# One product of q moved last, a closing bank of three steps instead of two, and w_mod loads spread over four iterations

## The chip, the cores and the metric

The kernel runs on one core of one Trainium2 chip. The metric is the time of one execution on the device in microseconds (us). Three runs of the kernel before the change took 440.44, 440.65 and 440.71 us; their median is 440.65 us. TensorE (PE) multiplies, VectorE (DVE) and ScalarE (ACT) do elementwise work, GpSimd (POOL) does small work and issues the accumulating DMAs, SyncE (SP) issues the plain ones. Nearly every wait below is one of these engines waiting for another, or for a DMA.

## The reference

One transformer block with adaLN conditioning: six vectors come from `silu(c) @ w_mod`, then a linear attention and a token-mixing MLP, each behind a modulated layer norm, are added to x. x is 2048 x 448, the hidden size of the MLP is 1792.

```
mod = (_silu(c) @ w_mod).reshape(c.shape[0], 6, 1, -1)
sa, ca, ga, sb, cb, gb = (mod[:, 0], ..., mod[:, 5])
h = _layernorm(x) * (1 + ca) + sa
x = x + ga * _A_ref(h, A_wqkv, A_wo)      # q, k, v; phi(t) = where(t>0, t+1, exp(t)) + 1e-6
h = _layernorm(x) * (1 + cb) + sb         # A: o = phi(q) (phi(k)^T v) / (phi(q) sum phi(k)), then @ wo
x = x + gb * _B_ref(h, B_w1, B_b1, B_w2, B_b2)   # B: gelu(LN(h)^T w1 + b1) w2 + b2, over tokens
```

## The kernel before

**Precision by parts.** PE works on operands rounded to a shorter form. Each f32 operand is cut into a high part (ACT copies it rounded) and a low part (full minus high), and a product becomes high x high, high x low and low x high, summed in one bank of PSUM. The low part is made in two ways: DVE subtracts, or ACT writes the negated high part and POOL issues a DMA that adds the full tile to it (an accumulating DMA). Names ending in h and l are such parts: `hh`, `hl` of the transposed normed tile, `wh`, `wl` of a weight, `pkh`, `pkl` of phi(k), `xh`, `xl` of the normed tile.

**The first stage** goes over the 16 token tiles of 128 rows (numbered from 0; the change's "tile 2" is the second tile, number 1 in the code). A head written out by hand treats tiles 0 to 2, then the loop at L594 runs t from 3 to 15. In iteration t PE makes k of tile t (`project`, eleven matmuls of 448 columns at L356), the transposes of tile t+1 (L325), and `a_outer(t - 3)`: phi(k)^T times the normed tile, eleven matmuls into four banks `cacc` (L453). `a_outer` reads `pkl` of tile t-3. That part is made in `a_pk_parts`, called with t-1 in iteration t: ACT writes the negated high part (L431) and POOL issues the adding DMA (L432). So `pkl` of tile 7 is issued in iteration 8 and read in iteration 10. POOL issues three accumulating DMAs in most iterations: `xl` (L404), `pkl` (L432) and the running sum of phi(k) into `pk` (L438); between them stand its small `rs` operations (L302), the reciprocal deviations of the norm.

**q of tile 1** is `project(1, 0, "qp", True)` at L582. With `late_low` its eleven products are sorted by a key: high x high weight chunks first, then low x high weight, then high x low weight (`wl0_0`, `wl0_1`, `wl0_2`), and at the end the two products of chunk 3, whose lower half holds both parts. `wl0_0` is made with an accumulating DMA (L226), `wl0_1` and `wl0_2` and the low rows of `wh0_3` by DVE (L213, L215).

**SP's queue.** SP issues the loads in the order of the code. A load waits for the last reader of the buffer that it is to fill; the buffers come from one pool of 76 slots, and whatever stands behind a waiting load in SP's queue waits too. In iteration t, `load_x(t + 4)` is issued, and in iterations 10 and 11 the four quarter loads of w_mod's vectors 4 and 3 (`load_mod`, L113). These vectors are used by DVE from iteration 11 on (L181, L183).

**The end.** The token mixer's second matrix is applied by `mult7` in blocks of seven steps. Each step multiplies by h with 448 columns (L1028) and by l with 224 (L1029). Of the very last block, the last `LAST = 2` steps go to a bank of their own, `yl` (`last7`, L1038): three matmuls of 224 columns each (L1043). DVE then adds both halves of the first bank `y` and the bank `yl` to the x tile `xb` (L1045, three additions), and SP stores it (L1046). Ahead of these three, DVE has the same kind of work for the block before: L1055 once and L1060 twice.

Of the kernel before, what the change touches and what calls it, by code (L numbers as in the profile page):

```python
# [30 lines left out]
DVE_LOW = (0, 1, 13, 14, 15)  # L31
AHEAD = 8
LAG = 5
LAST = 2
PRE2 = {16: (1, 0), 12: (1, 1), 8: (1, 2), 3: (4, 3), 1: (4, 4)}
MOD_AT = {11: [(4, 0)], 12: [(4, 1)], 13: [(4, 2)], 14: [(4, 3)], 15: [(3, 0), (3, 1)]}
QS = {0: 2, 4: 2}
WARM = 9
ACT_STATS = ()
PRE = 9  # L40
# [7 lines left out]
def block_kernel(ctx: ExitStack, tc: tile.TileContext, x, wqkv, wo, w1, b1, w2, b2, c, wmod, out):  # L48
# [26 lines left out]
    def bank(name):  # L75
        return psum.tile([P, 512], F32, name=name, tag="bank")
# [30 lines left out]

    wm = {}

    def load_mod(j):  # L110
        for k in range(4):
            wm[j, k] = (tslot if j == 5 else slot)(f"wm{j}_{k}", parts=G)
            nc.sync.dma_start(wm[j, k], wmod[k * G:(k + 1) * G, j * D:(j + 1) * D])  # L113

# [26 lines left out]
    def keep_warm(n):  # L141
        for i in range(n):
            nc.tensor.matmul(warm[:, :P], ones, ones, start=True, stop=True)
# [3 lines left out]
    nc.tensor.transpose(ct, c_sb, ident[:4, :4])  # L147
    keep_warm(WARM)

# [25 lines left out]
    def mod_part(j, k):  # L175
        if k == 0:
            macc[j] = (tslot if j == 5 else slot)(f"acc{j}", parts=G)
            if j == 5:
                nc.scalar.activation(macc[j], wm[j, 0], AF.Copy, scale=sc[:, 0:1])
            else:  # L180
                nc.vector.tensor_scalar_mul(macc[j], wm[j, 0], sc[:, 0:1])  # L181
        else:
            nc.vector.scalar_tensor_tensor(macc[j], wm[j, k], sc[:, k:k + 1], macc[j], op0=ALU.mult, op1=ALU.add)  # L183
# [12 lines left out]
    def mod_sum2(j):  # L196
        ps = bank(f"modp{j}")
        hi, lo = macc.pop(j)
        nc.tensor.matmul(ps[:, :D], ones_r[:G, :], hi, start=True, stop=False)
        nc.tensor.matmul(ps[:, :D], ones_r[:G, :], lo, start=False, stop=True)  # L200
        return ps
# [90 lines left out]
    def a_stats(t, b6=None):  # L292
        if t in ACT_STATS:
            a_rstd(t, a_mean(t))
            return
        b6 = a_moments(t) if b6 is None else b6
        mv = small.tile([P, 2], F32, name=f"mv{t}", tag="mv")
        nc.vector.bn_aggr(mv, b6)
        ve = small.tile([P, 1], F32, name=f"ve{t}", tag="ve")
        nc.vector.tensor_scalar_add(ve, mv[:, 1:2], EPS)  # L300
        rs = small.tile([P, 1], F32, name=f"rs{t}", tag="rs")
        nc.gpsimd.tensor_tensor(rs, ve, mhalf[:, 0:1], op=ALU.pow)  # L302
        st[t] = (mv[:, 0:1], rs)

    def a_norm_a(t):
        h = slot(f"h{t}", 512)
        nc.vector.scalar_tensor_tensor(h[:, :D], X[t], st[t][0], mods[1],
                                       op0=ALU.add if t in ACT_STATS else ALU.subtract, op1=ALU.mult)
        hs[t] = h

    def a_norm_b(t, sa=None):
        h = hs[t]
        nc.vector.scalar_tensor_tensor(h[:, :D], h[:, :D], st.pop(t)[1], mods[0] if sa is None else sa,
                                       op0=ALU.mult, op1=ALU.add)
# [6 lines left out]
    def a_transpose(t):  # L321
        h = hs[t]
        tps[t] = bank(f"tp{t}")
        for ch in range(4):
            nc.tensor.transpose(tps[t][:, ch * P:(ch + 1) * P], h[:, ch * P:(ch + 1) * P], ident)  # L325

    def a_split(t):
        hh = slot(f"hh{t}", 512, F32R)
        hl = slot(f"hl{t}", 512, F32R)
        split(tps.pop(t), hh, hl)  # L330
        heads[t] = (hh, hl)
# [11 lines left out]
    def project(t, j, name, late_low=False):  # L343
        hh, hl = heads[t]
        ps = bank(f"{name}{t}")
        o = ps[:, :D]
        todo = []
        for ch in range(4):
            a, b = (hh, ch, Whi[j, ch]), (hl, ch, Whi[j, ch])
            todo += [a, b] if ch == 3 else [a, (hh, ch, Wlo[j, ch]), b]  # L350
        if late_low:
            ws = [Wlo[j, ch] for ch in range(3)]
            key = lambda m: 3 if m[1] == 3 else 2 if any(m[2] is w for w in ws) else 0 if m[0] is hh else 1
            todo.sort(key=key)
        for n, (a, ch, b) in enumerate(todo):
            nc.tensor.matmul(o, a[:, ch * P:(ch + 1) * P], b, start=(n == 0), stop=(n == 10))  # L356
        return o
# [3 lines left out]
    def a_exp(t, ps):  # L361
        eks[t] = (slot(f"ek{t}"), slot(f"rk{t}"))
        nc.scalar.activation(eks[t][0], ps, AF.Exp)
        nc.scalar.activation(eks[t][1], ps, AF.Relu)
# [20 lines left out]
    def a_q(t):  # L385
        qps[t] = project(t, 0, "qp")
        del heads[t]

    def a_phi_q(keep=0):
        for t in sorted(qps)[:len(qps) - keep]:  # L390
            phi_q(qps.pop(t), f"q{t}", t)
            if t > QLATE:
                phi_q_sum(t)
# [21 lines left out]
    def a_high(t):  # L415
        a_high_act(t)
        a_high_low(t)
# [3 lines left out]
    def a_pk(t, ps):  # L421
        pkf[t] = phi_k(t, ps, tslot if t < 2 else slot)
# [21 lines left out]
    def a_outer(t):  # L444
        if not cacc:
            cacc.extend(bank(f"cacc{ch}") for ch in range(4))
        xh, xl = xss.pop(t)
        kh, kl = pks.pop(t)
        for ch in range(4):
            s = slice(ch * P, (ch + 1) * P)  # L450
            todo = [(xh, kh), (xh, kl)] + ([(xl, kh)] if ch < 3 else [])
            for i, (a, b) in enumerate(todo):
                nc.tensor.matmul(cacc[ch][:, :D], a[:, s], b, start=(t == 0 and i == 0),  # L453
                                 stop=(t == NT - 1 and i == len(todo) - 1))
# [139 lines left out]
    for t in range(3, NT):  # L594
        kp = project(t, 1, "kp")
        if t + 1 < NT:
            a_transpose(t + 1)
        a_outer(t - KV_LAG)
        if t in Q_EARLY:
            a_q(t)  # L600
        if t == 10:
            mp = mod_sum2(2)
        if t + 1 < NT:
            a_split(t + 1)
        if t + 2 < NT:
            a_norm_a(t + 2)

        for j, i in MOD_AT.get(t, ()):
            mod_part(j, i)
        if 11 <= t < 15:  # L610
            nc.vector.tensor_mul(wo_sb[t - 11], wo_sb[t - 11], mods[2][:G])
        a_exp(t, kp)
        if t + 2 < NT:
            a_norm_b(t + 2)
        a_pk(t, kp)
        a_phi_q()
        a_pk_parts(t - 1)
        if t + 3 < NT:
            a_stats(t + 3)
        if t + 2 < NT:  # L620
            a_dup(t + 2)
        if t == 3:
            a_high(3)
            a_high(4)
        if t + 2 < NT:
            a_high(t + 2)
        if t == 10:
            mod_out(2, mp)
        if t + 4 < NT:
            load_x(t + 4)  # L630
        if 5 <= t < 9:
            mod_part(2, t - 5)
        if t == 9:
            mod_split(2)
        if 5 <= t <= 5 + QLATE:
            phi_q_sum(t - 5)
        if t in (10, 11):
            load_mod(14 - t)
        if t == 4:
            for g in range(4):  # L640
                w = tslot(f"wo{g}", parts=G)
                nc.sync.dma_start(w, wo[g * G:(g + 1) * G, :])
                wo_sb.append(w)
            load_qkv(2, tslot)
            b1c = cst.tile([P, NF], F32, name="b1c")
            nc.sync.dma_start(b1c, b1.rearrange("(k p) -> p k", p=P))
            b2c = cst.tile([P, NT], F32, name="b2c")
            nc.sync.dma_start(b2c, b2.rearrange("(k p) -> p k", p=P))
        load_to(PRE_LOAD.get(t, 0))
# [205 lines left out]
    for i in range(NT + LAG):  # L855
# [6 lines left out]
        if 0 <= i - 1 < NT:  # L862
            b_out(i - 1)
        nq = min(len(late), QS.get(i, 1))
        for _ in range(nq):
            a_q(late.pop(0))
        t = i - LAG
# [146 lines left out]
    def mult7(q, m, r0, r1):  # L1014
# [6 lines left out]
        for r in range(r0, r1):  # L1021
            (h, l), i = hilo[q, m][r // 4], r % 4
            w, wh = uops[b, r]
            s = slice(i * P, (i + 1) * P)
            if (q, m) == (NP - 1, 6) and r >= PAIRS - LAST:
                last.append((h[:, s], l[:, s], w))
                continue
            nc.tensor.matmul(ps[:, :D], h[:, s], w, start=opens and r == r0, stop=False, skip_group_check=True)  # L1028
            nc.tensor.matmul(ps[:, :HD], l[:, s], wh, start=False,  # L1029
                             stop=closes and r == PAIRS - 1 - (LAST if (q, m) == (NP - 1, 6) else 0),  # L1030
                             skip_group_check=True)
# [6 lines left out]
    def last7():  # L1038
        x = X[NT - 1][:, :HD]
        ps = bank("yl")[:, :HD]  # L1040
        for i, (h, l, w) in enumerate(last):
            for n, (a, b) in enumerate(((h, w[:, :HD]), (h, w[:, HD:]), (l, w[:, :HD]))):
                nc.tensor.matmul(ps, a, b, start=i + n == 0, stop=n == 2 and i == LAST - 1)  # L1043
        for s in (acc2[NP - 1, 0][:, :HD], acc2[NP - 1, 0][:, HD:D], ps):
# [72 lines left out]
    k = NT  # L1117
# [24 lines left out]
    for o0, n in W1G[1:]:  # L1142
# [5 lines left out]
        for r in range(first, NT):  # L1148
# [4 lines left out]
            if xleft and k % 2:  # L1153
                t = xleft.pop(0)
# [11 lines left out]
    for q, m, r0, r1 in order:  # L1166
        if jobs:
            jobs.pop(0)()
        while xleft:
            t = xleft.pop(0)  # L1170
# [41 lines left out]
```

## Time and profile before

| what | value |
|---|---|
| median of 3 runs | 440.65 us (440.44 to 440.71) |
| the profiled execution | 440.77 us, of which the span from its first to its last instruction is 439.1 us |
| busy: PE, DVE, ACT, POOL | 433.9, 365.1, 266.9, 119.3 us |
| mean granted TensorE clock | 1.000 |
| DMA packets | 64.51 MB, mean 147 GB/s over the span |

Busy time is the time in which an engine's instructions run; waiting and issuing are not in it. Matmuls overlap: a row gives the duration of one, and the distance between two starts is shorter. The chain of waits follows the program back from its last instruction, at each step to what released it. A row of the timeline gives start, duration, engine, line, operation, output<-inputs, shape and count, and in brackets the idle time of that engine just before and what ended it. The view of windows gives for stretches of time each engine's busy time, the clock, the busy share of the DMA engines and what they moved; packets that overlap on an engine are both counted, so the share can be somewhat above 1.

### The profile page before, as it was taken

How to read it: one execution, taken by the hardware profiler on the slowest of the kernel's cores; microseconds unless marked ns; L12 is line 12 of the kernel's file. 1: busy time of each engine (PE TensorE's matmuls, PEld its weight loads, DVE VectorE, ACT ScalarE, POOL GpSimd, SP SyncE). 2: the span in 40 equal slices, each digit the busy share in tenths (PEclk: the TensorE clock that was granted, in tenths of full speed). 3: DMA queues.
4: the chain of work that ended last, by engine and by line, in shares of the span. 5: the costliest groups of instructions: out<-in, count | busy, mean ns of one | idle time of the engine just before them, and what ended most of it. 6: DMA issues, size and time to landing. Idle time of an engine off the chain costs nothing.

```text
span 439.1 us, 7288 instructions
## 1 busy us (share of the span) xinstructions
PE 433.9 (99%) x2394; PEld 402.4 (92%) x2394; DVE 365.1 (83%) x792; ACT 266.9 (61%) x570; POOL 119.3 (27%) x196
## 2 busy tenths in 40 slices
PE   8999999999999999999999999999999999999996
PEld 7689999999899999999999999999999999999996
DVE  5996898988898999997469586439999998898894
ACT  3778877655657777776766254236675555655550
POOL 2205775520024455664300000010112230231110
PEclk9999999999999999999999999999999999999999
DMA  8987999993441224222427546476667977977531
GB/s 233 303 213 117 181 197 230 221 258 102 138 100 26 47 47 123 50 50 60 132 69 237 177 143 186 131 194 187 151 143 191 177 172 176 188 161 208 75 52 34
DMA packets 65022, 64.51 MB, mean 147 GB/s; under 512 B 8472, under 2 KB 56792, under 8 KB 64984
## 3 DMA queue, kind: packets, MB, share of 16 engines
q1 hardware_dynamic: 54608, 47.62, 36.8%
q0 software_dynamic: 10368, 16.42, 23.8%
q8 instruction: 19, 0.31, 0.3%
q14 instruction: 19, 0.16, 0.1%
q10 hardware_dynamic: 8, 0.00, 0.0%
HBM read 41.88 MB, written 7.34 MB: 112 GB/s over the span
## 4 chain that ended last, share of the span: by engine, by line
PE 95%; DMA 3%; DVE 1%; ACT 0%; issue 0%; SPq 0%; DVEq 0%
PE y L1028 19%; PE up L829 10%; PE up L828 10%; PE up L830 10%; PE y L1029 9%; PE op L778 8%; PE cacc L453 8%; PE qp L356 7%; PE kp L356 7%; DMA wl<-wr 2%; PE tq L758 2%; PE tp L325 1%; DMA wm<-in_w_mod_dram 1%; PE kvb L691 1%; PE wp L846 1%; PE colp L475 0%
## 5 line engine op out<-in xcount | busy, mean ns | idle before, releaser
L829 PE MATMUL up<-h2l,ph 128*128 128x448 f32 x224 | 81.3, 363 | 0.0
L828 PE MATMUL up<-h2h,ph 128*128 128x448 f32 x224 | 81.2, 362 | 0.0
L830 PE MATMUL up<-h2h,pl 128*128 128x448 f32 x224 | 80.7, 360 | 0.0
L988 POOL DMA_DIRECT2D a<-a x16 | 14.1, 948 | 145.5 <-DMA a<-in_B_w_dram 97.8
L828 PEld LDWEIGHTS up<-h2h,ph 128*128 128x128 f32 x224 | 42.0, 188 | 3.3
L830 PEld LDWEIGHTS up<-h2h,pl 128*128 128x128 f32 x224 | 41.9, 187 | 3.0
L829 PEld LDWEIGHTS up<-h2l,ph 128*128 128x128 f32 x224 | 42.0, 188 | 2.1
L80 DVE TENSOR_TENSOR pl<-pr,ph 128x512 fp32r<-128x512 f32 x48 | 32.3, 686 | 11.5 <-ACT ph L79 8.6
L79 ACT ACTIVATE ph<-pr 128x512 fp32r<-128x512 f32 x48 | 29.1, 627 | 17.8 <-PE up L829 7.4
L1050 ACT ACTIVATE cc<-y 128x448 f32<-128x448 f32 x24 | 13.0, 544 | 22.9 <-PE y L1029 22.9
L453 PE MATMUL cacc<-pkh,xh 128*128 128x448 f32 x64 | 24.3, 379 | 0.0
L453 PE MATMUL cacc<-pkl,xh 128*128 128x448 f32 x64 | 23.2, 363 | 0.0
L778 PE MATMUL op<-oh,pth 128*128 128x448 f32 x60 | 23.0, 383 | 0.0
L1071 POOL DMA_DIRECT2D out_dram<-yt x14 | 12.9, 921 | 34.9 <-DVE yt L1057 25.4
L778 PE MATMUL op<-oh,ptl 128*128 128x448 f32 x60 | 21.7, 362 | 0.0
L356 PE MATMUL qp<-wh,hh 128*128 128x448 f32 x60 | 21.6, 365 | 0.0
L356 PE MATMUL qp<-wh,hl 128*128 128x448 f32 x60 | 21.4, 362 | 0.0
L356 PE MATMUL kp<-wh,hl 128*128 128x448 f32 x56 | 20.3, 363 | 0.0
L356 PE MATMUL kp<-wh,hh 128*128 128x448 f32 x56 | 20.2, 362 | 0.0
L736 POOL TENSOR_SCALAR den<-den 128x16 f32<-128x16 f32 x16 | 8.6, 536 | 39.2 <-DVE den L733 39.1
L763 ACT ACTIVATE pth<-tq 128x512 fp32r<-128x512 f32 (+1 forms) x16 | 9.6, 599 | 15.7 <-PE tq L758 15.6
L302 POOL TENSOR_TENSOR rs<-ve,mhalf 128x1 f32<-128x1 f32 x16 | 13.9, 869 | 18.8 <-DVE ve L300 18.5
(234 smaller groups left out, 1356.9 us busy)
## 6 DMA issues: line engine op xcount, KB each, us to landing
pr<-in_B_w_dram SPq DMA_DIRECT2D x56, 256.0 KB, 2.9
a<-in_B_w_dram SPq DMA_DIRECT2D x32, 256.0 KB, 4.3
a<-in_B_w_dram SPq DMA_DIRECT2D x32, 192.0 KB, 4.2
wm<-in_w_mod_dram SPq DMA_DIRECT2D x24, 196.0 KB, 4.9
x<-in_A_x_dram SPq DMA_DIRECT2D x16, 224.0 KB, 4.0
out_dram<-x SPq DMA_DIRECT2D x14, 224.0 KB, 2.0
out_dram<-yt POOLq DMA_DIRECT2D x14, 224.0 KB, 4.5
pk<-pk POOLq DMA_DIRECT2D x12, 224.0 KB, 4.7
```

Of the source, the lines that this page charges most:

```text
L79: nc.scalar.activation(hi, full, AF.Copy)
L80: nc.vector.tensor_sub(lo, full, hi.bitcast(F32))
L302: nc.gpsimd.tensor_tensor(rs, ve, mhalf[:, 0:1], op=ALU.pow)
L356: nc.tensor.matmul(o, a[:, ch * P:(ch + 1) * P], b, start=(n == 0), stop=(n == 10))
L453: nc.tensor.matmul(cacc[ch][:, :D], a[:, s], b, start=(t == 0 and i == 0), stop=(t == NT - 1 and i == len(todo) - 1))
L778: nc.tensor.matmul(opb[t][:, :D], a[:, g * P:(g + 1) * P], b, start=(n == 0), stop=(n == len(todo) - 1))
L828: nc.tensor.matmul(ps[:, :D], hi[:, sl], mh, start=first, stop=False)
L829: nc.tensor.matmul(ps[:, :D], hi[:, sl], ml, start=False, stop=False)
L830: nc.tensor.matmul(ps[:, :D], lo[:, sl], mh, start=False, stop=last)
L988: nc.gpsimd.dma_start(w, a, accum_op=ALU.add)
L1028: nc.tensor.matmul(ps[:, :D], h[:, s], w, start=opens and r == r0, stop=False, skip_group_check=True)
L1029: nc.tensor.matmul(ps[:, :HD], l[:, s], wh, start=False, stop=closes and r == PAIRS - 1 - (LAST if (q, m) == (NP - 1, 6) else 0), skip_gro ...
```

## The change

Three edits that don't touch each other. A constant more stands at the top, so lines from 38 on move down by one.

```diff
-LAST = 2
+LAST = 3
...
+MOD_LOAD = {8: (4, (0, 1)), 9: (4, (2, 3)), 10: (3, (0, 1)), 11: (3, (2, 3))}
...
-    def load_mod(j):
-        for k in range(4):
+    def load_mod(j, ks=range(4)):
+        for k in ks:
             wm[j, k] = (tslot if j == 5 else slot)(f"wm{j}_{k}", parts=G)
...
-            key = lambda m: 3 if m[1] == 3 else 2 if any(m[2] is w for w in ws) else 0 if m[0] is hh else 1
+            key = lambda m: 3 if m[1] == 3 else 4 if m[2] is ws[0] else 2 if any(m[2] is w for w in ws) else 0 if m[0] is hh else 1
...
-        if t in (10, 11):
-            load_mod(14 - t)
+        if t in MOD_LOAD:
+            load_mod(*MOD_LOAD[t])
```

**q of tile 1, on PE** (output `qp1`; `wh0_c`, `wl0_c` are the high and low parts of q's weight chunk c, `hh1` and `hl1` those of the tile). Before:

```order
L356 MATMUL qp1_403<-wh0_2_295,hl1_263 128x448
L356 MATMUL qp1_403<-wl0_0_272,hh1_262 128x448
L356 MATMUL qp1_403<-wl0_1_314,hh1_262 128x448
L356 MATMUL qp1_403<-wl0_2_357,hh1_262 128x448
L356 MATMUL qp1_403<-wh0_3_297,hh1_262 128x448
L356 MATMUL qp1_403<-wh0_3_297,hl1_263 128x448
L356 MATMUL qp2_427<-wh0_0_270,hh2_324 128x448
```

and now:

```order
L357 MATMUL qp1_403<-wh0_2_295,hl1_263 128x448
L357 MATMUL qp1_403<-wl0_1_314,hh1_262 128x448
L357 MATMUL qp1_403<-wl0_2_357,hh1_262 128x448
L357 MATMUL qp1_403<-wh0_3_297,hh1_262 128x448
L357 MATMUL qp1_403<-wh0_3_297,hl1_263 128x448
L357 MATMUL qp1_403<-wl0_0_272,hh1_262 128x448
L357 MATMUL qp2_427<-wh0_0_270,hh2_324 128x448
```

The product with `wl0_0` moves from the seventh place to the eleventh; the four behind it move up by one. The next projection, `qp2`, starts at the same place.

**The loads in SP's queue** (`x12` to `x15` are token tiles, `wm4_k` and `wm3_k` the quarters of w_mod's vectors 4 and 3). Before:

```order
L106 DMA x12_930<-in_A_x_dram 128x448
L106 DMA x13_995<-in_A_x_dram 128x448
L106 DMA x14_1067<-in_A_x_dram 128x448
L113 DMA wm4_0_1069<-in_w_mod_dram 112x448
L113 DMA wm4_1_1071<-in_w_mod_dram 112x448
L113 DMA wm4_2_1073<-in_w_mod_dram 112x448
L113 DMA wm4_3_1075<-in_w_mod_dram 112x448
L106 DMA x15_1141<-in_A_x_dram 128x448
L113 DMA wm3_0_1143<-in_w_mod_dram 112x448
L113 DMA wm3_1_1145<-in_w_mod_dram 112x448
L113 DMA wm3_2_1147<-in_w_mod_dram 112x448
L113 DMA wm3_3_1149<-in_w_mod_dram 112x448
```

and now:

```order
L107 DMA x12_930<-in_A_x_dram 128x448
L114 DMA wm4_0_933<-in_w_mod_dram 112x448
L114 DMA wm4_1_935<-in_w_mod_dram 112x448
L107 DMA x13_999<-in_A_x_dram 128x448
L114 DMA wm4_2_1005<-in_w_mod_dram 112x448
L114 DMA wm4_3_1007<-in_w_mod_dram 112x448
L107 DMA x14_1075<-in_A_x_dram 128x448
L114 DMA wm3_0_1077<-in_w_mod_dram 112x448
L114 DMA wm3_1_1079<-in_w_mod_dram 112x448
L107 DMA x15_1145<-in_A_x_dram 128x448
L114 DMA wm3_2_1147<-in_w_mod_dram 112x448
L114 DMA wm3_3_1149<-in_w_mod_dram 112x448
```

`x13` has two w_mod loads ahead of it that it did not have and `x14` four; between `x14` and `x15` stand two instead of four, and two instead of four come behind `x15`. Because the loads ask for buffers earlier, most buffers of the pool go to other tiles from iteration 8 to 15. In the changed program `wm4_0` takes the buffer that phi(k) of tile 4 (`pk4`) leaves, and waits for the sum DMA (L438) that reads it; `wm4_1` takes that of the normed tile `h7` and waits for the `xl` DMA of tile 7; `x13` waits for a matmul of PE's `a_outer(4)`; `wm4_2` takes that of `h8` and waits for the `xl` DMA of tile 8; `x14` and `wm3_0` take those of the two inputs of phi(k) of tile 8 (DVE, L369), `wm3_1` one that DVE leaves in the same iteration.

**The end, on PE** (`y_0` is the first bank, `yl` the closing one; the left operand is the moving half of u, the right the weight part). Before:

```order
L1029 MATMUL y_0_5394<-ut_3_3677,a22l_0_5463 128x224
L1028 MATMUL y_0_5394<-ut_4_3811,a22h_4_5466 128x448
L1029 MATMUL y_0_5394<-ut_4_3811,a22l_4_5467 128x224
L1043 MATMUL yl<-ut_5_3934,a22h_4_5466 128x224 x2
L1043 MATMUL yl<-ut_5_3934,a22l_4_5467 128x224
L1043 MATMUL yl<-ut_6_4057,a22h_4_5466 128x224 x2
L1043 MATMUL yl<-ut_6_4057,a22l_4_5467 128x224
```

and now:

```order
L1030 MATMUL y_0_5394<-ut_3_3677,a22l_0_5463 128x224
L1044 MATMUL yl<-ut_4_3811,a22h_4_5466 128x224 x2
L1044 MATMUL yl<-ut_4_3811,a22l_4_5467 128x224
L1044 MATMUL yl<-ut_5_3934,a22h_4_5466 128x224 x2
L1044 MATMUL yl<-ut_5_3934,a22l_4_5467 128x224
L1044 MATMUL yl<-ut_6_4057,a22h_4_5466 128x224 x2
L1044 MATMUL yl<-ut_6_4057,a22l_4_5467 128x224
```

The first bank closes one step earlier; that step is now three matmuls of 224 columns in the closing bank, in place of one of 448 and one of 224. The order on DVE, ACT and POOL does not change.

## Prediction

> **What bounds the kernel now.** I read the page's busy times and the chain of waits first.
>
> ```profile
> PE 433.9 (99%) x2394; PEld 402.4 (92%) x2394; DVE 365.1 (83%) x792; ACT 266.9 (61%) x570; POOL 119.3 (27%) x196
> PE 95%; DMA 3%; DVE 1%; ACT 0%; issue 0%; SPq 0%; DVEq 0%
> ```
>
> PE is busy for 433.9 of 439.1 us and 95% of the chain is PE's. So an edit can gain only where PE stands still, and a stop that it adds is paid in full to the end, since PE has no idle time in which to catch up. The chain's one long DMA, in order of time:
>
> ```profile
> 17.43 8.12 DMA wl<-wr
> ...
> 25.60 3.48 PE qp L356 x16
> ```
>
> The low part `wl0_0` of q's first weight chunk lands at 17.43 + 8.12 = 25.55, and PE goes on at 25.60. That is the wait which the new order of q avoids. The other edits work at 50 to 78 us (loads) and in the last 3 us.
>
> **q of tile 1.** PE's timeline there:
>
> ```profile
> 24.75 0.77 PE L356 MATMUL qp<-wh,hl 128*128 128x448 f32 x3
> ...
> 25.60 0.88 PE L356 MATMUL qp<-wl,hh 128*128 128x448 f32 x3
> 26.31 0.36 PE L356 MATMUL qp<-wh,hh 128*128 128x448 f32 x1
> ...
> 26.71 0.36 PE L356 MATMUL qp<-wh,hh 128*128 128x448 f32 x1
> ```
>
> Running matmuls start 0.20 apart (26.31 to 26.71 is two). The three from 24.75 could be followed by the next at 24.75 + 3 x 0.20 = 25.35; it came at 25.60, a stop of 0.25. The three behind it took 26.31 - 25.60 = 0.71 instead of 0.60, 0.11 of restart. In the new order the seventh product reads `wl0_1`, the eighth `wl0_2`, then `wh0_3`. DVE makes the last two:
>
> ```profile
> 22.87 0.62 DVE L213 TENSOR_TENSOR wl<-wr,wh 128x448 fp32r<-128x448 f32 x1
> 23.52 0.62 DVE L215 TENSOR_TENSOR wh<-wr,wh 64x448 fp32r<-64x448 f32 x1
> ```
>
> Ready at 23.49 and 24.14, 1.2 us before 25.35. `wl0_0` is now wanted at 25.35 + 4 x 0.20 = 26.15, 0.6 after its landing. So the stop goes: `qp2` starts near 26.35 instead of 26.71. **Term 1: -0.35** at this place (nothing at worst, if the low part lands 0.6 later; 0.36 at best). ACT's exponential waits for the eleventh product as before, and gets it earlier.
>
> **The closing bank.** DVE's and PE's timelines at the end:
>
> ```profile
> 433.24 0.62 DVE L1055 TENSOR_TENSOR cc<-y,cc 128x448 f32<-128x448 f32 x1 [0.65 <-PE y L1029]
> 433.90 0.82 DVE L1060 TENSOR_TENSOR xb<-cc,xb 128x224 f32<-128x224 f32 x2
> 434.80 0.82 DVE L1045 TENSOR_TENSOR xb<-y,xb 128x224 f32<-128x224 f32 x2
> 435.72 0.39 DVE L1045 TENSOR_TENSOR xb<-yl,xb 128x224 f32<-128x224 f32 x1
> ```
>
> ```profile
> 434.19 0.27 PE L1029 MATMUL y<-ut,a22l 128*128 128x224 f32 x1
> ...
> 434.50 0.26 PE L1029 MATMUL y<-ut,a22l 128*128 128x224 f32 x1
> ...
> 435.16 0.28 PE L1043 MATMUL yl<-ut,a22l 128*128 128x224 f32 x1
> ```
>
> `y` closes at 434.76 now and one step earlier, at 434.46, after the change. But DVE is in the additions of L1060 until 434.72; its next can start at about 434.75, not at 434.46. So the three last additions move by 0.05, the third to 435.67. The bank it reads closes at 435.44 now; a step in it costs three matmuls of 224 columns for 448 + 224, the same columns with one start more, and 0.03 more would make it 435.47, still in time. **Term 2: -0.05** (from +0.03, if that start counts, to -0.31, one whole step, if DVE were free).
>
> **The loads.** The trace gives them a place where PE already waits. PE in iterations 9 and 10, and the adding DMA that makes `pkl` of tiles 6 and 7 (the row "DMA to landing" belongs to the issue above it):
>
> ```profile
> 65.29 0.36 PE L453 MATMUL cacc<-pkl,xh 128*128 128x448 f32 x1
> 65.49 0.36 PE L453 MATMUL cacc<-pkh,xl 128*128 128x448 f32 x1
> ...
> 70.13 0.44 PE L453 MATMUL cacc<-pkl,xh 128*128 128x448 f32 x1
> 70.41 0.36 PE L453 MATMUL cacc<-pkh,xl 128*128 128x448 f32 x1
> ```
>
> ```profile
> L432 POOL DMA_DIRECT2D pkl<-pk x1: 841/841/841, 58.5 to 58.5; - x1
> DMA to landing us min/median/max: 4.2/4.2/4.2
> ...
> L432 POOL DMA_DIRECT2D pkl<-pk x1: 864/864/864, 63.4 to 63.4; - x1
> DMA to landing us min/median/max: 6.7/6.7/6.7
> ```
>
> Tile 6's part lands at 62.7, 2.5 before its reader at 65.29. Tile 7's lands at 70.1 and is read at 70.13: no margin, and that product is followed after 0.28 instead of 0.20, so 0.08 is lost already. If PE arrives 0.35 earlier it waits there. **Term 1 therefore reaches the end only if this DMA lands earlier too; the loads decide.** They share the DMA engines with it:
>
> ```profile
> 52.00:56.00 4.00, 4.00 (x24) 3.72 (x23) 3.50 (x10) 2.90 (x7) 3.45 (x6) 1.00 1.04 194
> 56.00:60.00 4.00, 4.00 (x22) 3.71 (x21) 3.83 (x10) 3.33 (x8) 2.75 (x4) 1.00 1.06 192
> 60.00:62.00 2.00, 2.00 (x13) 1.89 (x12) 2.00 (x6) 1.58 (x4) 1.53 (x3) 1.00 1.11 193
> 62.00:64.00 2.00, 2.00 (x11) 1.88 (x11) 1.90 (x4) 1.58 (x4) 1.43 (x2) 1.00 0.90 153
> ...
> 76.00:78.00 2.00, 2.00 (x12) 1.87 (x11) 1.89 (x4) 1.97 (x5) 1.24 (x2) 1.00 1.08 298
> ```
>
> The last two columns are the DMA share and GB/s. The engines are full from 52 on, before any of these eight loads, except for 62 to 64. So a load that goes out earlier takes its time from the adding DMAs behind it. At the 298 GB/s of the stretch that is nearly all loads, 196 KB take 0.67 us.
>
> When do they go out? From these rows (SP's timeline, then POOL's DMAs by tile):
>
> ```profile
> 52.92 10.03 SPq L106 DMA_DIRECT2D x<-in_A_x_dram  x3
> 63.05 5.33 SPq L113 DMA_DIRECT2D wm<-in_w_mod_dram  x4
> ```
>
> ```profile
> L438 POOL DMA_DIRECT2D pk<-pk x1: 875/875/875, 51.2 to 51.2; - x1
> DMA to landing us min/median/max: 4.0/4.0/4.0
> ...
> L404 POOL DMA_DIRECT2D xl<-h x1: 1761/1761/1761, 52.2 to 52.2; - x1
> DMA to landing us min/median/max: 4.7/4.7/4.7
> ...
> L404 POOL DMA_DIRECT2D xl<-h x1: 890/890/890, 57.2 to 57.2; - x1
> DMA to landing us min/median/max: 4.4/4.4/4.4
> ```
>
> Now `x12` to `x14` go out at 52.92 to 62.62, and four quarters of vector 4 from 63.05 to 67. In the new queue `wm4_0` needs the buffer freed by the sum DMA of tile 4, 51.2 + 4.0 = 55.2, `wm4_1` that of `xl` of tile 7, 52.2 + 4.7 = 56.9, `wm4_2` and `wm4_3` that of `xl` of tile 8, 57.2 + 4.4 = 61.6. `x14` waits for DVE's phi(k) of tile 8 and goes out near 63.8, 1 us later than now, with two quarters of vector 3 right behind. So the burst ahead of tile 7's part isn't thinned: between 61.6 and 66 there are again `x14` and four w_mod loads, and two more have gone before it. What is thinned is the burst after 72, where no product of PE waits.
>
> Two loads more ahead of the part: 2 x 0.67 = 1.34. Against that stands what is free: 62 to 64 has a share of 0.90 where its neighbours reach about 1.07, 0.17 x 2 us = 0.34. And POOL's next DMA starts 0.3 after a landing where the landing holds it:
>
> ```profile
> 70.37 0.87 POOL L432 DMA_DIRECT2D pkl<-pk  x1 [2.64 <-ACT mh L79]
> ```
>
> (POOL stood idle for 2.64 and went on 0.3 after 70.1). Tile 7's issue at 63.37 comes 0.6 after the landing at 62.7, so 0.3 of it was not the DMAs' and covers as much. Left: 1.34 - 0.34 - 0.3 = 0.7. The part lands at 70.8 and PE passes 0.7 later than now, term 1 gone in the wait. **Term 3, with term 1 inside: +0.7.** Bounds: if the part lands before 69.7, the gain of 0.35 and the lost 0.08 stay, -0.43; if the two loads of vector 3 also get ahead and nothing is free, 4 x 0.67 = +2.7. I take the middle, since the early pair is certain by the order and the buffers, and the rest depends on turns. Behind the late DMA, POOL's queue holds the next two and tile 12's `rs`, for which DVE's norm waits; all move by the same 0.7, as PE does, so I add nothing. Other tiles now take other buffers of the pool; on PE, DVE and ACT I cost that at nothing, since the pool of 76 covers more than two iterations (from 65.29 to 70.13, 4.84, is one) and no row of theirs waits for a buffer now; if that cover is gone, the wait shows as an idle engine in iterations 8 to 15.
>
> The trace shows that the turns matter, not how. The Trainium skill, "DMA: Bandwidth & Descriptors", section "Queues, rings and completion order", says that each DMA engine goes round robin between the queues it has work for. By that, a longer line of SP's loads can't take more than its turns, so the early pair counts and the burst doesn't: the lower half of the range. By that page's section "Bandwidth", 436 GB/s, a load is an estimate of 0.46 and the pair 0.92, and the sum would be about +0.2; the row's 298 GB/s is used.
>
> **Sum.** 440.77 (span 439.1 and 1.67 around it, which no edit touches) + 0.7 - 0.05 = 441.4 for the profiled execution. That execution is 0.12 above the median of 440.65, so I forecast **441.3** (+0.15%). About 0.2%, 0.88 us, is what a measurement can tell from no change.
>
> **The rivals.** (a) *The spread works*: tile 7's part lands by 69.7, because six of the eight loads leave its neighbourhood. For: its 6.7 us against 4.2 fall together with the burst at 63 to 67. Against: four w_mod loads and `x14` still stand at 61.6 to 66. Then -0.43 - 0.05: **440.2**. Chance 0.23. (b) *A wash*: the part lands within 0.3 of now; the early pair fills holes that the share doesn't show, and PE gives term 1 back in iteration 10, so the q edit does nothing. **440.6**, chance 0.12. (c) *The loads crowd it out*, the other side: SP's loads get more than their turn, as at 76 to 78 with 298 GB/s, and the two quarters of vector 3 pass as well. It decides from a landing of 71 on. One such load more on the forecast: 0.7 + 0.67 - 0.05 = 1.3, two 2.0; I take 1.7: **442.3**, chance 0.25. (d) *Forecast*: 441.3, own range 440.9 to 441.7, chance 0.40.
>
> **How the numbers follow.** Slower by over 0.2% (above 441.53): (c) and about 0.06 from the top of (d), 0.31. Faster by over 0.2% would need 0.88 where the places named hold 0.48: 0.02. The rest, 0.67, is within. The range reaches from (a)'s 440.15 to 442.6, in which most of (c) lies.
>
> **What would show it.** Right: no idle time of PE at `wl0_0`, `qp2` at 26.35; DVE's last addition 0.05 closer to its neighbours; tile 7's `pkl` still about 7 us from issue to landing, and PE's product at 70.8 after a wait of about 1 us. Wrong: that part landing in under 6 us, with PE 0.4 ahead at 71 (a); or a wait of 2 us there or at the transposes behind it (c). A wait anywhere else in 27 to 117 us would make the account of the margins wrong.

## The result, and the profile after

The changed kernel takes **441.81 us** (median of 18 runs, 440.74 to 442.31), the kernel before 440.71 in 18 runs beside it. The ratio is **1.0017**, 95% interval 1.0010 to 1.0024: slower, by little. By the ratio this is 0.75 us, by the medians 1.10; single runs of each of the two spread over about 1.5 us, so the two need not agree. The profiled execution took 441.83 us (span 440.1), 1.06 more than the profiled one of before.

The page of the changed kernel: busy times, the chain by engine and line, and one group of instructions (its last two numbers are PE's idle time ahead of that group and what ended it):

```profile
PE 434.0 (99%) x2395; PEld 402.7 (92%) x2395; DVE 364.8 (83%) x792; ACT 266.6 (61%) x570; POOL 119.3 (27%) x196
...
PE 92%; POOL 2%; DMA 2%; issue 2%; DVE 1%; ACT 1%; POOLq 0%; DVEq 0%
PE y L1029 19%; PE up L830 10%; PE up L829 10%; PE up L831 10%; PE y L1030 9%; PE op L779 8%; PE qp L357 8%; PE cacc L454 6%; PE kp L357 4%; DMA pkl<-pk 2%; PE tq L759 2%; PE warm L144 1%; PE tp L326 1%; PE kvb L692 1%; PE wp L847 1%
...
L454 PE MATMUL cacc<-pkl,xh 128*128 128x448 f32 x64 | 23.4, 366 | 1.6 <-DMA pkl<-pk 1.6
```

The chain's long DMA is no longer `wl<-wr` of q but `pkl<-pk`. PE has one idle stretch that it didn't have, in iteration 10, as PE's timeline shows:

```profile
69.26 0.45 PE L454 MATMUL cacc<-pkh,xh 128*128 128x448 f32 x1
71.34 0.48 PE L454 MATMUL cacc<-pkl,xh 128*128 128x448 f32 x1 [1.63 <-DMA pkl<-pk]
71.66 0.36 PE L454 MATMUL cacc<-pkh,xl 128*128 128x448 f32 x1
```

Elsewhere the second of these products comes 0.28 after the first. Here it comes 2.08 after it, a stop of 1.80, and 0.12 is lost to the restart (71.66 - 71.34 is 0.32 instead of 0.20). Before, the first of these products stood here:

```profile
69.84 0.45 PE L453 MATMUL cacc<-pkh,xh 128*128 128x448 f32 x1
```

So PE came to it 0.58 sooner in the changed kernel (69.84 - 69.26) and had to wait longer. The adding DMA of tile 7:

```profile
L433 POOL DMA_DIRECT2D pkl<-pk x1: 867/867/867, 64.3 to 64.3; - x1
...
DMA to landing us min/median/max: 7.0/7.0/7.0
```

It lands at 71.30, **1.24 later** than before (70.06): it goes out 0.93 later and takes 0.31 longer. The later issue comes from the same part of tile 6, two rows in the changed kernel's trace:

```profile
L433 POOL DMA_DIRECT2D pkl<-pk x1: 1086/1086/1086, 58.5 to 58.5; - x1
DMA to landing us min/median/max: 5.5/5.5/5.5
```

Tile 6's part landed at 63.99, and POOL's DMA for tile 7 went out 0.31 behind that, as it does in all six kernels that send loads in iteration 8 and have this DMA (0.31 or 0.32). Before, tile 6's part landed at 62.77 and held nothing up: POOL waited for ACT until 63.37. Measured from PE, the issue is later still. Before, and in the five other traces without loads in iteration 8, the part goes out 6.47 or 6.48 before PE's first product of iteration 10 (69.84 - 63.37); in the changed kernel it is 4.96 (69.26 - 64.30). This 1.51 makes up most of the stop of 1.80.

What was put ahead of the part can be counted. The view of DMA queues for the stretch from 52 to the landing (packets, MB, share of 16 engines), first before (52 to 70.06), then after (52 to 71.3); q0 are POOL's adding DMAs, q1 the plain loads:

```profile
q0 software_dynamic: 1586, 2.42, 82.5%
q1 hardware_dynamic: 816, 1.29, 22.1%
```

```profile
q0 software_dynamic: 1561, 2.38, 76.4%
q1 hardware_dynamic: 1196, 1.89, 29.5%
```

The adding DMAs moved about the same; the loads moved 0.60 MB more, the bytes of **three** loads of 196 KB. Most of that is not due to the longer stretch: at 70.06 the loads of the changed kernel had moved 1.84 MB already. Their share is 22.1% of 18.06 = 3.99 us before and 29.5% of 19.3 = 5.69 now, so 1.70 us more on all engines, 0.57 a load. SP's timeline shows them:

```profile
55.82 1.21 SPq L114 DMA_DIRECT2D wm<-in_w_mod_dram  x2
57.13 0.43 SPq L107 DMA_DIRECT2D x<-in_A_x_dram  x1
62.84 1.08 SPq L114 DMA_DIRECT2D wm<-in_w_mod_dram  x2
64.50 0.35 SPq L107 DMA_DIRECT2D x<-in_A_x_dram  x1
64.95 1.56 SPq L114 DMA_DIRECT2D wm<-in_w_mod_dram  x2
```

The early pair at 55.8, and then five loads between 62.84 and 66.2, around the part's issue at 64.30. Before, the burst there was `x14` and four quarters too, but its last two went out only at 66.6 and 67.0.

q of tile 1 and the end of the program, PE's and DVE's timelines:

```profile
23.65 0.86 PE L357 MATMUL qp<-wh,hh 128*128 128x448 f32 x3
24.35 0.76 PE L357 MATMUL qp<-wh,hl 128*128 128x448 f32 x3
24.95 0.56 PE L357 MATMUL qp<-wl,hh 128*128 128x448 f32 x2
...
25.75 0.36 PE L357 MATMUL qp<-wl,hh 128*128 128x448 f32 x1
25.95 0.36 PE L357 MATMUL qp<-wh,hh 128*128 128x448 f32 x1
```

```profile
435.13 0.82 DVE L1061 TENSOR_TENSOR xb<-cc,xb 128x224 f32<-128x224 f32 x2
435.87 0.81 DVE L1046 TENSOR_TENSOR xb<-y,xb 128x224 f32<-128x224 f32 x2
436.78 0.39 DVE L1046 TENSOR_TENSOR xb<-yl,xb 128x224 f32<-128x224 f32 x1
```

```profile
436.42 0.28 PE L1044 MATMUL yl<-ut,a22l 128*128 128x224 f32 x1
```

From the start of `qp1` to that of `qp2` it is 25.95 - 23.65 = 2.30; before it was 26.71 - 24.05 = 2.66. The stop is gone, -0.36 against this one execution of before. At the end, PE's last matmul starts 1.26 later than before (435.16), DVE's last addition only 1.06 later (435.72): the closing bank gives back about 0.2.

### The profile page after: what moved, and what is told of

It reads as the page before. It is cut to its first block, busy times and chain, and to the rows that moved or that the text cites. A ratio compares the mean times of both kernels' runs of the same rounds, so it can differ in the third digit from the quotient of the medians.

```text
span 440.1 us, 7286 instructions
## 1 busy us (share of the span) xinstructions
PE 434.0 (99%) x2395; PEld 402.7 (92%) x2395; DVE 364.8 (83%) x792; ACT 266.6 (61%) x570; POOL 119.3 (27%) x196
## 4 chain that ended last, share of the span: by engine, by line
PE 92%; POOL 2%; DMA 2%; issue 2%; DVE 1%; ACT 1%; POOLq 0%; DVEq 0%
PE y L1029 19%; PE up L830 10%; PE up L829 10%; PE up L831 10%; PE y L1030 9%; PE op L779 8%; PE qp L357 8%; PE cacc L454 6%; PE kp L357 4%; DMA pkl<-pk 2%; PE tq L759 2%; PE warm L144 1%; PE tp L326 1%; PE kvb L692 1%; PE wp L847 1%
## 5 line engine op out<-in xcount | busy, mean ns | idle before, releaser
L1051 ACT ACTIVATE cc<-y 128x448 f32<-128x448 f32 x24 | 13.0, 545 | 22.1 <-PE y L1030 22.1
```

## The experiments

Each kernel was timed in five rounds beside the kernel before on the same chip (8 to 12 runs of it, 15 to 32 of before), the changed one as above. "Landing" is that of tile 7's `pkl`, "stop" PE's stop for it beyond the usual 0.28, "plain MB" what the loads moved from 52 to the landing, all three in the one profiled execution of each kernel, which took between 0.45 less and 0.95 more than the median of that kernel.

| kernel | median, before's | ratio (95%) | landing | stop | plain MB |
|---|---|---|---|---|---|
| before | | | 70.06 | 0 | 1.29 |
| the change | 441.81, 440.71 | 1.0017 (1.0010 to 1.0024) | 71.30 | 1.80 | 1.89 |
| q alone | 440.60, 440.86 | 0.9997 (0.9988 to 1.0006) | 69.80 | 0 | 1.30 |
| loads alone | 441.82, 440.86 | 1.0020 (1.0010 to 1.0031) | 71.31 | 0.99 | 1.89 |
| closing bank alone | 440.81, 440.86 | 0.9998 (0.9989 to 1.0007) | 70.53 | 0 | 1.28 |
| q and loads | 442.11, 440.81 | 1.0026 (1.0015 to 1.0037) | 70.80 | 1.09 | 1.89 |
| change, tile 7's part by DVE | 440.31, 440.86 | 0.9991 (0.9982 to 1.0000) | - | 0 | - |
| early pair only | 440.86, 440.83 | 1.0007 (0.9998 to 1.0015) | 69.26 | 0 | 1.12 |
| all earlier still | 442.00, 440.83 | 1.0028 (1.0016 to 1.0041) | 71.26 | 0 | 2.23 |
| change, vector 3 as before | 440.87, 440.81 | 1.0002 (0.9993 to 1.0011) | 70.38 | 0.20 | 1.49 |
| q and closing bank | 440.33, 440.83 | 0.9995 (0.9986 to 1.0003) | 67.86 | 0 | 1.09 |
| the same again | 440.34, 440.81 | 0.9992 (0.9984 to 1.0001) | 69.20 | 0 | 1.21 |
| these two, later loads | 440.54, 440.83 | 0.9996 (0.9986 to 1.0006) | 69.50 | 0 | 1.09 |
| these two, tile 7's part by DVE | 440.44, 440.87 | 0.9987 (0.9978 to 0.9996) | - | 0 | - |

**One edit at a time.** Three kernels have one of the three edits each:

```diff
# q alone
-            key = lambda m: 3 if m[1] == 3 else 2 if any(m[2] is w for w in ws) else 0 if m[0] is hh else 1
+            key = lambda m: 3 if m[1] == 3 else 4 if m[2] is ws[0] else 2 if any(m[2] is w for w in ws) else 0 if m[0] is hh else 1
# loads alone
+MOD_LOAD = {8: (4, (0, 1)), 9: (4, (2, 3)), 10: (3, (0, 1)), 11: (3, (2, 3))}
# closing bank alone
-LAST = 2
+LAST = 3
```

> Only the order of q is changed. Theory (the transfer of tile 7's pkl bounds iteration 10): qp2 starts 0.36 us closer to the start of qp1 (2.30 instead of 2.66), the transfer still lands near 70.1, PE waits there for 0.3 to 0.4 us, and the time stays at 440.7 (within 0.15). Rival (PE's arrival drives that transfer, so it comes earlier too): the 0.36 reaches the end, 440.35.

> Only the spread loads; q's order and the closing bank as before. Theory: the transfer of tile 7's pkl lands near 71.3, whenever PE arrives, and PE's wait is about 1.3 us (1.88 less what q had gained); the end is later by the full 1.2: 441.9. Rival (most of the loss comes of PE being earlier, which sends out the other transfers earlier and closer together): the landing is at 70.8 or sooner, 441.4 or less.

> Only the closing bank with three steps. Theory from the trace of the changed kernel: DVE's third addition starts 0.36 after PE's last matmul starts instead of 0.56, so 0.20 is gained: 440.5. Rival (the size on record, DVE held by the additions before): 0.05, 440.65.

*q alone.* `qp2` starts 2.29 after `qp1`, as expected. But the theory that the transfer's landing stands still fell: it landed at 69.80 and PE, 0.29 earlier than before, found it there, if only just (the product behind it comes 0.31 later, not 0.20).

```profile
69.55 0.45 PE L454 MATMUL cacc<-pkh,xh 128*128 128x448 f32 x1
69.84 0.47 PE L454 MATMUL cacc<-pkl,xh 128*128 128x448 f32 x1
70.15 0.37 PE L454 MATMUL cacc<-pkh,xl 128*128 128x448 f32 x1
```

With the old loads the adding DMAs move along with PE: this one went out at 63.07 instead of 63.37, in both cases 6.47 or 6.48 ahead of PE. The median is 0.26 lower (0.13 by the ratio), which the interval doesn't tell from nothing.

The gain at this place is not 0.36 in every execution, though. In the nine traces with the new order `qp2` starts 2.29 or 2.30 after `qp1`. In the five with the old order it starts 2.66 (before), 2.57 (all earlier still), 2.49 (early pair only), 2.40 (closing bank alone) and 2.29 (loads alone) after it. So the stop that the new order avoids was anything from 0 to 0.36, 0.19 in the mean, and the profiled execution of before had the largest. In the loads alone `wl0_0` landed at 25.15, before PE wanted it, and PE's timeline shows no stop:

```profile
25.12 0.76 PE L357 MATMUL qp<-wh,hl 128*128 128x448 f32 x3
25.72 0.76 PE L357 MATMUL qp<-wl,hh 128*128 128x448 f32 x3
...
26.71 0.36 PE L357 MATMUL qp<-wh,hh 128*128 128x448 f32 x1
```

*Loads alone.* The whole loss is here: a landing at 71.31 and 0.96 by the medians.

```profile
70.08 0.45 PE L454 MATMUL cacc<-pkh,xh 128*128 128x448 f32 x1
71.35 0.47 PE L454 MATMUL cacc<-pkl,xh 128*128 128x448 f32 x1 [0.82 <-DMA pkl<-pk]
```

PE came to this product 0.82 later than in the changed kernel (70.08 against 69.26), and they went on at 71.35 and 71.34. Between these two executions the earlier PE only waited longer. PE's wait was expected at about 1.3 and came out at 0.99. *The closing bank* shows in its trace what it shows in the changed kernel: from PE's last start to DVE's last addition it is 436.09 - 435.73 = 0.36, where before it was 435.72 - 435.16 = 0.56. Its 0.2 can't be seen in the times (0.05, with an interval of 0.4 to either side).

**q and the loads together**, the changed kernel with `LAST = 2`:

```diff
-LAST = 3
+LAST = 2
```

> The changed kernel with the closing bank of two steps again: the order of q and the spread loads together. Theory (with the spread loads the DMA engines are full from 52 to the landing, so the part comes at 71.3 by the clock, however early PE is): landing at 71.3 as in the two runs with these loads, PE's wait 1.6 to 1.9, q's gain lost in it; the time is that of the loads alone within 0.2, 441.8. Rival (landing follows PE, as in the run of q alone): 0.3 less than the loads alone, 441.5 or below.

The time goes with the theory and not with the rival: 442.11 is 0.3 above the loads alone, where 0.2 to either side was expected, the two intervals overlap widely, and no gain of q is to be seen. The landing and the wait don't go with it: 70.80 in place of 71.3, and a stop of 1.09 in place of 1.6 to 1.9. PE came to the product at 69.47, 0.61 sooner than in the loads alone, and the part landed 0.51 sooner. So "71.3 by the clock" doesn't hold. What moves the landing by these tenths, and whether q's gain is lost in every execution with these loads, stays open; the times only show that none of it is seen.

**Without the transfer.** In the changed kernel DVE makes tile 7's low part, so this DMA doesn't exist:

```diff
-PK_LOW = (9,)
+PK_LOW = (7, 9)
```

> The changed kernel, with the low part of phi(k) of tile 7 made by DVE's subtraction, as tile 9's is, in place of the adding DMA. Theory (this one transfer carries the whole loss): no wait in iteration 10, and the gains of q (0.36), of the 0.08 lost there before, and of the closing bank (0.20) reach the end: 440.05, 0.65 below before. Rival (the crowd only moves on to tile 8's part or to the norm behind POOL's queue): a new wait of 0.5 to 1.5 in iterations 11 to 13, 440.6 to 441.6.

By the medians the time goes from 1.10 above before to 0.55 below (0.40 by the ratio); 0.65 below was expected. Without this transfer the loss is gone. That doesn't take the transfer away alone: the DMA engines have 224 KB less to move, and since buffers come free at other times, the second quarter of vector 3's pair behind `x14` went out only at 71.88. So the loss passes through this transfer; how much of it the crowd would cost elsewhere isn't shown. The wait at the transposes that the rival spoke of is there, but small:

```profile
73.98 0.36 PE L357 MATMUL kp<-wh,hl 128*128 128x448 f32 x1
74.45 0.63 PE L326 MATMUL tp<-ident,h 128*128 128x128 f32 x4
```

0.47 instead of the usual 0.21: PE waits 0.26 for a normed tile.

**Which loads.** Three kernels send the pairs at other times; the first two have q and the closing bank as before, the third as changed:

```diff
# early pair only
+MOD_LOAD = {8: (4, (0, 1)), 10: (4, (2, 3)), 11: (3, (0, 1, 2, 3))}
# all earlier still
+MOD_LOAD = {8: (4, (0, 1, 2, 3)), 9: (3, (0, 1)), 10: (3, (2, 3))}
# change, vector 3 as before
+MOD_LOAD = {8: (4, (0, 1)), 9: (4, (2, 3)), 11: (3, (0, 1, 2, 3))}
```

> Only one pair of loads is moved: the first two quarters of vector 4 go out in iteration 8, the other six loads stay where they were before; q and the closing bank as before. Theory (what counts is how many loads reach the DMA engines ahead of tile 7's pkl, and that number is the old one): the part lands near 70.1, at most 0.3 after PE gets there, and the time stays at 440.86 within 0.2. Rival (a pair that goes out in 55 to 58 pushes the adding DMAs back for good): the part lands near 71, 441.6.

> All four quarters of vector 4 in iteration 8, vector 3 in iterations 9 and 10; q and the closing bank as before. Theory (each load ahead of tile 7's pkl costs its time on the DMA engines, 0.67 less what is free): about two loads more ahead than with the spread of the change alone, the part lands near 72.6 and the time is 443 (2.2 over before). Rival (the turns between the queues hold the loads back, more of them make no difference): as with the spread alone, 441.8.

> The changed kernel, but vector 3's first pair of quarters goes out with its second one in iteration 11, as before; vector 4 is spread over iterations 8 and 9, q and the closing bank as changed. Theory (in the traces 594 KB more of plain loads pass before tile 7's pkl lands, three loads and not the two of the forecast, and the third is made up of the pair of vector 3 that goes out right behind x14, beside the part): without that pair the landing comes 1.3 to 2 sooner than 71.3, so at 69.3 to 70.0, PE waits at most 0.6, and the time is 440.3 to 440.7. Rival (the early pair at 55 to 57 carries the loss): the landing stays near 71, 441.6.

*Early pair only.* No stop at this product, and no change of the time that can be measured; in the profiled execution, 0.44 above the median, PE lost another 0.28 between 80 and 90. The part goes out late, as in the changed kernel, but lands after 4.5:

```profile
L433 POOL DMA_DIRECT2D pkl<-pk x1: 867/867/867, 64.7 to 64.7; - x1
...
DMA to landing us min/median/max: 4.5/4.5/4.5
```

So the pair does push the adding DMAs back (64.75 against 63.37), but behind it the next load left at 65.66 and the next quarters at 67.33, after the part was on its way. *Vector 3 as before* takes away just the pair behind `x14`: landing 70.38, two loads fewer ahead of it (1.49 against 1.89 MB), and of the 1.10 that the medians had lost 0.06 is left.

```profile
69.94 0.45 PE L454 MATMUL cacc<-pkh,xh 128*128 128x448 f32 x1
70.42 0.48 PE L454 MATMUL cacc<-pkl,xh 128*128 128x448 f32 x1
```

The landing was expected somewhat sooner (69.3 to 70.0) and the time at 440.7 or less. In this execution, 0.95 above its kernel's median, PE stood still once more, at the transposes of a later iteration:

```profile
85.58 0.66 PE L326 MATMUL tp<-ident,h 128*128 128x128 f32 x4 [0.55 <-DVE h L314]
```

DVE waited there 1.15 for POOL's `rs`, and `rs` stood behind a sum DMA that went out only at 83.39, 0.31 behind the landing of an earlier one.

Each of these two kernels lacks a part of the change, and neither has the loss. With the early pair the part goes out at 64.17 to 65.14, without it at 62.95 to 64.01. With the pair behind `x14` it then takes 6.5 to 7.0, without that pair 6.2 and 4.5. So the early pair delays the part, and the pair behind `x14` keeps the crowd in its way. No kernel sends the pair behind `x14` without the early one, so that both are needed is shown from one side only.

*All earlier still* refutes the simple price of 0.67 for each load ahead, as far as the landing goes. The loads moved 2.23 MB ahead of the landing, 0.34 more than in the changed kernel, yet it came at 71.26, not 72.6. The median is 442.0, not 443, though the profiled execution, the slowest of eight, took 442.95. The adding DMAs moved less in that time (2.24 MB, against 2.45 with the loads alone). POOL's next sum DMA went out only at 68.54 (66.52 with the loads alone), again 0.31 behind a landing, and `rs` stands behind it. So PE's stop moved to what depends on that, a normed tile for the transposes, as the timelines of POOL, DVE and PE show:

```profile
68.54 0.84 POOL L439 DMA_DIRECT2D pk<-pk  x1 [2.54 <-issue]
```

```profile
70.00 0.69 DVE L314 SCALAR_TENSOR_TENSOR h<-h,rs,mod 128x448 f32<-128x448 f32 x1 [2.61 <-POOL rs L303]
```

```profile
69.34 0.37 PE L357 MATMUL kp<-wh,hl 128*128 128x448 f32 x1
70.74 0.66 PE L326 MATMUL tp<-ident,h 128*128 128x128 f32 x4 [1.03 <-DVE h L314]
```

**What is left to gain.** The order of q and the closing bank without the spread loads, twice; the same with loads two at a time from iteration 10 to 13; and the same with the old loads and tile 7's part by DVE:

```diff
# all four: the key of q as changed, LAST = 3
# q and closing bank, and again
+MOD_LOAD = {10: (4, (0, 1, 2, 3)), 11: (3, (0, 1, 2, 3))}
# later loads
+MOD_LOAD = {10: (4, (0, 1)), 11: (4, (2, 3)), 12: (3, (0, 1)), 13: (3, (2, 3))}
# tile 7's part by DVE: the loads of the first, and
+PK_LOW = (7, 9)
```

> The order of q and the closing bank of three steps, the loads as before. Theory (without the extra loads that transfer follows PE, so q's gain is kept, and the closing bank's too): 0.3 and 0.2 less, 440.4. Rival (the transfer's landing is fixed, q's gain is lost in iteration 10): 440.65.

> The same as q_last, the order of q and the closing bank of three steps with the loads as before, once more beside these two. Theory: 0.5 below before, 440.35, and faster than both of the kernels compared; no wait of PE over 0.3 between 27 and 117. In q_last tile 7's pkl landed at 67.9 and in q_alone, with the same loads, at 69.8; a third landing shows how far it scatters between executions. Rival (q_last's profile was a lucky one): landing at 69.8 to 70.1, with a time of 440.6.

> The order of q, the closing bank of three steps, and the eight loads two at a time in iterations 10 to 13, so later than before. Theory (two loads fewer ahead of tile 7's pkl): it lands near 69, PE doesn't wait, and the whole 0.36 + 0.08 + 0.20 is kept: 440.2. Rival (the loads now crowd the transfers and DVE's uses of vector 4 in iterations 11 to 14): a wait of 0.5 to 1 between 72 and 90, 440.7 to 441.2.

> The order of q and the closing bank of three steps, the loads as before, and the low part of phi(k) of tile 7 made by DVE instead of the adding DMA. Theory (with the old loads PE no longer waits for that part, so there is nothing left to take away; DVE's additional subtraction may cost what it cost with the spread loads, a wait of 0.3 at the transposes): 440.35 to 440.6. Rival (in some executions the part still lands late, which one profile doesn't show): 440.1 or below, and a higher share of executions under 440.2.

None of the four has a stop of PE over 0.05 between 27 and 117 beyond those that every tile has. All medians lie 0.29 to 0.50 under before (0.18 to 0.57 by the ratios). To be had were 0.56 where the stop at q is the full 0.36, and 0.39 with its mean of 0.19. The first pair is 0.50 and 0.47 lower by the medians, with both intervals just reaching 1; the later loads, expected at 440.2, gain nothing more; only the last one's interval excludes 1 (0.13% faster), though its median is no lower than the first's. So dropping the spread loads beats the changed kernel plainly (ratios of 0.9995 and 0.9992 against 1.0017, with intervals that lie apart), and the kernel before by about what can be measured. A part that still lands late in some executions was not found; in the two profiled executions of the same kernel it came at 67.86 and 69.20.

## Why the prediction came out where it did

The forecast was 441.3; the measured 441.81 is 0.5 above it and inside the whole range, but 0.11 above the forecast's own range of 440.9 to 441.7. By the ratio the loss is 0.17%, by the forecast 0.15%. Some of this nearness is luck: term 2 was 0.15 too small a gain and term 3 about 0.5 too small a loss, and the two errors offset each other in part.

- **What bounds the kernel**: right. PE is 1.25 later behind the stop in iteration 10 (71.66 against 70.41) and 1.26 later at its last matmul; nothing is caught up between.
- **Term 1, q**: -0.35 forecast, -0.36 measured against the profiled execution of before. The working is right for that execution, but it read the largest of the five stops in the traces with the old order; in the others it is 0 to 0.28. That the gain is swallowed in iteration 10 fits the changed kernel, where PE came 0.58 sooner and passed 1.25 later, and no time with the spread loads shows the gain. The sentence that it reaches the end only if this DMA lands earlier is right, but the DMA does: without the spread loads it came at 69.80, 67.86 and 69.20 in three executions. What the forecast took as a fixed landing follows PE, as long as the adding DMAs aren't held up by loads: the part's issue stays 6.47 or 6.48 ahead of PE.
- **Term 2, the closing bank**: -0.05 forecast, about -0.2 measured in all traces, inside the bounds. The mis-sized step is "its next can start at about 434.75". The first of the last additions had been waiting for `y`. Freed of that, it starts 0.74 behind the start of the pair ahead (435.13 to 435.87); before it was 0.90 (433.90 to 434.80). The record's end at 434.72 was taken for the time at which the next may start. The last addition now waits for PE's closing bank (436.42 + 0.28 = 436.70, then 436.78), so little more is to be had there; no run has a bank of four steps.
- **Term 3, the loads**: the place, the sign and the mechanism were right, the size was not: +0.7 forecast for the landing with q's gain inside, +1.24 measured. The term that was mis-sized is "two loads more ahead": it was three, 1.29 to 1.89 MB. The pair of vector 3 was put "right behind" `x14` but counted for nothing, since the burst had as many loads as before; yet in the old burst the last two waited for their buffers until 66.6 and 67.0, and in the new one all five were out by 66.2. With three, the forecast's own terms give 3 x 0.67 - 0.34 - 0.3 = 1.4, near the 1.24; with the 0.57 that a load took here, between its prices of 0.67 and 0.46, they give 1.1. The cover of 0.3 held: tile 6's part landed 1.22 later, and tile 7's issue moved by 0.93. The kernel without that pair says the same: landing 0.9 sooner, time back at that of before. That the price holds load by load is refuted by the kernel with all loads earlier still.
- **The turns**: the prediction weighed the rule of the Trainium skill, "DMA: Bandwidth & Descriptors", section "Queues, rings and completion order", that each DMA engine goes round robin between the queues it has work for. The prediction concluded that a longer line of loads would take no more than its turns, and that the burst would not count. The burst counts: without the pair behind `x14` most of the loss is gone. The queues of the changed kernel from 63.3 to 70:

```profile
q0 software_dynamic: 440, 0.66, 64.1%
q1 hardware_dynamic: 613, 0.97, 42.3%
```

  613 plain packets against 440 adding ones, where it was 523 against 490 before: by packets the loads had more than every second turn, in both kernels. POOL had two or three DMAs under way through that whole stretch (the landings and issues of the changed kernel's trace), so its queue as a whole was not empty; whether it was empty on single engines can't be seen, since the packets of the trace don't say which engine moved them. So this neither bears the rule out nor refutes it.
- **The rivals**: (a) and (b) are out, since the landing came later. The truth lies between (d) and (c): the landing of 71.30 meets (c)'s condition of 71, with the mechanism that (c) named (the quarters of vector 3 pass as well), and the price of one load more that it starts from (0.7 + 0.67 - 0.05 = 1.3; measured 1.06 in the profiled execution). The 1.7 that it took was too much.
- **What would show it**: no idle time at `wl0_0` and 7.0 us from issue to landing came as foretold; PE's wait was 1.8 and not 1, nearer to the 2 us that the prediction named as a sign of (c), partly because this execution was 0.40 ahead already at `qp1` (23.65 against 24.05), which the wait swallowed as well. One small stop that wasn't foreseen stands at 49.97 (0.02 and a restart of 0.1, for `pkl` of tile 3).

## What to carry to other kernels

Spreading loads helps only if the stretch that they move into has DMA time left, and if what is behind it has slack: look for the DMA that lands with no margin and count the bytes that pass ahead of it, before and after, by when each load's buffer comes free and not by how many loads stand in the queue. A gain that is upstream of such a DMA is kept while that DMA's issue follows the engine that gained, and lost once other transfers hold it up. Edits of a few tenths should be timed alone: here one edit's loss hid two gains, and these are plain in the traces but hardly in the times. And a stop read from one trace is that execution's: q's was 0 to 0.36 in five.

## What the runs showed of the hardware that was not expected

- With the same instructions ahead, the head takes a different time in each execution. The first product of k starts at 11.91 in the changed kernel's trace and at 12.94 in that of the closing bank alone; the fourteen traces fill the space between. It goes with the first loads: the last quarter of the second w_mod vector landed at 9.71 and 10.74. Single runs of one kernel spread over 1.0 to 2.6 us; how much of that is the head isn't shown, since one execution in each set was traced.

```profile
11.91 0.92 PE L503 MATMUL kp<-wr,h0t 128*128 128x448 f32 x2
```

```profile
12.94 0.92 PE L503 MATMUL kp<-wr,h0t 128*128 128x448 f32 x2
```

- By the time that their packets take, adding DMAs are dear: from 52 to the landing before, 2.42 MB of them took 82.5% of 16 engines and 1.29 MB of plain loads 22.1%. For each MB that is twice as much (34% against 17% of the stretch).
- A DMA's time from issue to landing says little by itself: tile 7's part took 4.5 to 7.0 us in these traces, and the kernel with the lowest value (4.5, early pair only) was no faster than before; the part had gone out 1.4 later there.
- In all fourteen traces, from 20 to 120, POOL never had more than three DMAs under way, and no issue came sooner than 0.25 behind the landing of the third DMA before it; 17 to 25 of the 30 or so in a trace came within 0.4 of it, most often at 0.31 (63.99 to 64.30, 71.30 to 71.61). What stands behind a held issue on POOL, the small `rs` too, waits with it. Whether the chip or the program sets the three isn't shown.
